# An attention and channel-mix kernel: the last but one input group of its head loaded and cast in halves, and casting loads released one group later

## The chip, the cores and the metric

The kernel runs on one core of a Trainium2 chip. The metric is the device time of the program in microseconds (us), as the median of several executions. The profile shows one execution; its span is about 1.8 us shorter than the time of the same execution, so spans are compared with spans and times with times.

The engines are PE (TensorE, matrix products), PEld (its weight loads), DVE (VectorE), ACT (ScalarE), POOL (GpSimd) and SP (SyncE, which here only issues transfers).

## The reference

Two layers run one after the other, with B = 4, N = 6208, C = 256 and a hidden width of 1024:

```python
# cross-covariance attention
qn = q / (norm(q, axis=1) + 1e-6);  kn = k / (norm(k, axis=1) + 1e-6)
s  = kn.transpose(0, 2, 1) @ qn / tau          # 256 x 256 for each batch
a  = softmax(s, axis=-1)
x  = v @ a
# channel mix
xk = mu_k * x + (1 - mu_k) * x_prev            # x_prev: x shifted by one row
xr = mu_r * x + (1 - mu_r) * x_prev
out = sigmoid(xr @ w_r) * (relu(xk @ w_k)**2 @ w_v)
```

The softmax of a batch needs all rows of its q and k. So batch 0's q and k have to be read first: this is the *head*. From then on (the *body*) the kernel works on blocks of 512 rows of v and takes the sums of the next batch along.

## The kernel before

Rows are taken in groups of 512: twelve of them (`NB = 12`; g = 0 to 11, called k0 to k11 and q0 to q11 below) and a rest of 64 rows (k12). A k piece of the head is a load in fp32, a cast to bf16 on DVE, squares on ACT, products on PE, and one piece later the sums of the squares on PE:

```python
def k_piece(g, s0, s1, last=False):            # s0:s1 of the four 128-row parts of group g
    f = head_load(k, 0, g, s0, s1)             # DMA issued by SP; 8 buffers
    kt = pq.tile([P, S, C], BF16, name="kb", tag="kb", bufs=6)
    nc.vector.tensor_copy(kt[:rows, :n], f[:rows, :n])                 # L141, the cast
    sq = ...
    nc.scalar.activation(sq[:rows, :n], f[:rows, :n], AF.Square)       # L143
    ...  nc.tensor.matmul(s_ps0[:, ih, :], kt[...], qb[g][...])        # L146, s += k^T q
    flush()                                    # L113: norm matmuls of the piece before
```

A q piece looks the same, without the products but with `filler(FQ, g)`: three matmuls (L192) whose result nobody reads, which keep PE busy. The order in the head, and the lines that the change edits:

```python
order += [("k", NB)] + [("k", g) for g in range(NB - LEAD, NB - 1)]   # k12, k4 ... k10
for what, g in order:
    ...
        kt = k_piece(g, 0, rows_of(g)[1])
        ...
        if g == NB - LEAD + 2:
            nc.vector.tensor_copy(rq_bc0, bc_ps)       # the q norms; used by the softmax
        if g == NB - 2:                                # after k10
            nc.sync.dma_start(mu_k_t, ...)             # 2 x 256 values of 4 bytes
            nc.sync.dma_start(mu_r_t, ...)
        if g == NB - 5:                                # k7: the gate
            nc.gpsimd.tensor_copy(gate, kt[:, 0, 0:1]) # POOL waits here for k7's cast ...
            v_load(0)                                  # ... and then issues the casting loads
            nc.gpsimd.dma_start(w_k_sb, ...)
            v_load(1); v_load(2); more_rows(1)
k_piece(NB - 1, 0, 2)                                  # k11 in three pieces
k_piece(NB - 1, 2, 3)
k_piece(NB - 1, 3, 4, last=True)
flush()
```

After the head come the softmax (L157 opens it), the transposes of v's first two blocks on PE (L247), the first block's x (L273), and then the body, which opens with block 0's products with w_k (L339) and block 1's x matmul (L258).

Of the kernel before, what the change touches and what calls it, by code (L numbers as in the profile page):

```python
# [18 lines left out]
def kernel(  # L19
# [21 lines left out]
    NB = N // M  # L41
# [40 lines left out]
    def rows_of(g):  # L82
        return (P, S) if g < NB else (L, 1)
# [5 lines left out]
    LEAD = 8  # L89
# [3 lines left out]
    def head_load(t, b, g, s0, s1):  # L93
        rows = rows_of(g)[0]
        f = pq.tile([P, S, C], F32, name="f", tag="f4", bufs=NF)
        nc.sync.dma_start(f[:rows, :s1 - s0], src_rows(t, b, g, s0, s1))
        return f
# [6 lines left out]
    def first(key):  # L104
        if key in started:
            return False
        started.add(key)
        return True
# [9 lines left out]
    def flush():  # L118

        while pend:  # L120
            norm_mm(*pend.pop(0))

    def q_piece(g, last=False):
        rows, n = rows_of(g)
        f = head_load(q, 0, g, 0, n)
        qt = pq.tile([P, S, C], BF16, name="qb", tag="b2", bufs=NB + 1)
        qb[g] = qt
        nc.vector.tensor_copy(qt[:rows, :n], f[:rows, :n])
        sq = pq.tile([P, S, C], BF16, name="hsq", tag="hsq", bufs=5)
        nc.scalar.activation(sq[:rows, :n], f[:rows, :n], AF.Square)  # L130
        flush()
        pend.append((nq_ps, "q", sq, rows, n, last))
        if g < NB:
            filler(FQ, g)

    def k_piece(g, s0, s1, last=False):
        rows, n = rows_of(g)
        n = s1 - s0
        f = head_load(k, 0, g, s0, s1)
        kt = pq.tile([P, S, C], BF16, name="kb", tag="kb", bufs=6)  # L140
        nc.vector.tensor_copy(kt[:rows, :n], f[:rows, :n])  # L141
        sq = pq.tile([P, S, C], BF16, name="hsq", tag="hsq", bufs=5)
        nc.scalar.activation(sq[:rows, :n], f[:rows, :n], AF.Square)  # L143
        for s in range(n):
            for ih in range(2):
                nc.tensor.matmul(s_ps0[:, ih, :], kt[:rows, s, ih * P:(ih + 1) * P], qb[g][:rows, s0 + s, :],  # L146
                                 start=first("s"), stop=last and s == n - 1, skip_group_check=True)
        flush()
        pend.append((nk_ps, "k", sq, rows, n, last))
        return kt  # L150

    def root(src, n):
        a = pn.tile([P, 4], F32, name="nrm_a")
        if len(src.shape) == 3:
            nc.vector.tensor_reduce(a[:, :n], src, axis=AX, op=OP.add)
        else:
            nc.vector.tensor_copy(a[:, :n], src)  # L157
        r = pn.tile([P, 4], F32, name="nrm_r")
        nc.gpsimd.tensor_tensor(r[:, :n], a[:, :n], half[:, :n], op=OP.pow)
        return r  # L160

    def inverse(r, n):

        nc.vector.tensor_scalar_add(r[:, :n], r[:, :n], 1e-6)
        o = pn.tile([P, 4], F32, name="nrm_o")
        nc.vector.reciprocal(o[:, :n], r[:, :n])
        return o
# [3 lines left out]
    def spread(r):  # L171
        w = pn.tile([P, 3, 2], BF16, name="rw", bufs=1)
        d = pn.tile([P, 2], F32, name="rd", bufs=1)
        nc.vector.tensor_copy(w[:, 0], r[:, :2])
        nc.vector.tensor_tensor(d, r[:, :2], w[:, 0], op=OP.subtract)
        nc.vector.tensor_copy(w[:, 1], d)
        nc.vector.tensor_tensor(w[:, 2], d, w[:, 1], op=OP.subtract)
        return w

    def broadcast(w, tag, **kw):  # L180
        bc_ps = ps.tile([P, 2, P], F32, name="bc_ps", tag=tag, **kw)
        for h in range(2):
            for u in range(3):
                nc.tensor.matmul(bc_ps[:, h], w[:, u, h:h + 1].to_broadcast([P, P]), ident,
                                 start=h == 0 and u == 0, stop=u == 2, skip_group_check=True)
        return bc_ps.rearrange("p h d -> p (h d)")
# [37 lines left out]
    def v_load(i):  # L224
        b, t = blocks[i]
        v_bf = pq.tile([P, S, C], BF16, name="v_bf", tag="b2", bufs=NB + 1)
        nc.gpsimd.dma_start(v_bf, v[b, t * M:(t + 1) * M, :].rearrange("(s p) c -> p s c", p=P))  # L227
        st[i, "v"] = v_bf
# [184 lines left out]
    def group_load(b, g):  # L413
        rows, n = rows_of(g)
        qk = pq.tile([P, S, 2, C], BF16, name="qk", tag="qk", bufs=5)
        groups[b, g] = {"qk": qk}
        for i, t in enumerate((q, k)):
            nc.gpsimd.dma_start(qk[:rows, :n, i], src_rows(t, b, g))  # L418
# [112 lines left out]
    def more_rows(n):  # L531
        while pos["load"] < min(len(loads), n):
            group_load(*loads[pos["load"]])
            pos["load"] += 1

    loads = [(b, g) for b in range(1, B) for g in GORD]
    order = [("q", NB)] + [("q", g) for g in range(LEAD)]
    for g in range(LEAD, NB):
        order += [("k", g - LEAD), ("q", g)]
    order += [("k", NB)] + [("k", g) for g in range(NB - LEAD, NB - 1)]  # L540
    for what, g in order:
        if what == "q":
            q_piece(g, last=g == NB - 1)
        else:
            kt = k_piece(g, 0, rows_of(g)[1])
            if g == NB:
                nq = root(nq_ps, 2)
            if g == NB - LEAD + 1:
                bc_ps = broadcast(spread(inverse(nq, 2)), "v", bufs=2)
            if g == NB - LEAD + 2:  # L550
                nc.vector.tensor_copy(rq_bc0, bc_ps)
            if g == NB - 2:
                nc.sync.dma_start(mu_k_t, moe_mu_k.rearrange("(h p) -> p h", p=P))
                nc.sync.dma_start(mu_r_t, moe_mu_r.rearrange("(h p) -> p h", p=P))
            if g == NB - 5:
                nc.gpsimd.tensor_copy(gate, kt[:, 0, 0:1])
                v_load(0)
                nc.gpsimd.dma_start(w_k_sb, moe_w_k.rearrange("(ko ki) f -> ki ko f", ki=P))
                v_load(1)
                v_load(2)  # L560
                more_rows(1)
    k_piece(NB - 1, 0, 2)
    k_piece(NB - 1, 2, 3)
    k_piece(NB - 1, 3, 4, last=True)
# [40 lines left out]
    for i in range(-2, NBLK):  # L605
        for j in range(8):
# [58 lines left out]
            for u in due.get(T, []):  # L665
                b, g, s = units[u]
# [48 lines left out]
```

## Time and profile before

| | before |
|---|---|
| time, median of 3 | 511.66 us (511.42 to 511.71) |
| span of the profiled execution | 509.72 us |
| PE busy | 493.9 us, 97% |
| first matmul of k7 to last norm matmul of k | 32.78 to 38.64 us |
| last norm matmul of k to block 1's first x matmul | 7.03 us |
| block 1's first x matmul to the last matmul of all | 459.53 us |

Beside what the prediction quotes, three views are needed for the comparison, the third behind the prediction. The first is PE's timeline at the end of the head (start in us, duration, engine, line, operation, out and inputs, sizes, number of instructions):

```profile
34.74 0.34 PE L113 MATMUL nk_ps<-ones_b,hsq 128*128 128x1 bf16 x8
...
35.82 0.34 PE L113 MATMUL nk_ps<-ones_b,hsq 128*128 128x1 bf16 x8
36.30 1.05 PE L146 MATMUL s_ps<-qb,kb 128*128 128x256 bf16 x8
```

The eight norm matmuls take 0.20 us of PE's issue (34.74 to 34.95, where the next group starts: no pause). After those of 35.82 the next group, k10's, starts only at 36.30: this is the hole of which the prediction speaks. The second view is PE's timeline where the body opens:

```profile
43.66 0.62 PE L247 MATMUL vT_ps<-ident,v_bf 128*128 128x128 bf16 x8 [0.21 <-DMA v_bf<-in_v_dram]
...
44.98 0.59 PE L339 MATMUL kT_ps<-xk,w_k_sb 128*128 128x512 bf16 x2
45.66 0.39 PE L258 MATMUL xT_ps<-vT,a_sb 128*128 128x512 bf16 x1
```

PE waits for v1's landing; from there its own instructions run on to block 1's x matmul at 45.66. The third is a row of SP's own waits in the last 5 us: the wait for the last stores of the result, us in total, times, longest.

```profile
SPq L710 <- DMA out_dram<-res: 1.8, 1, 1.8
```

### The profile page before, as it was taken

Reading aid. Unit: us, or ns where it says so; the run is one execution under the profiler, and the core shown is the slowest. Engines: PE = TensorE matmul, PEld = TensorE weight load, DVE = VectorE, ACT = ScalarE, POOL = GpSimd, SP = SyncE. Lnnn points to the kernel's source line nnn. Section 1 sums busy time; section 2 is a strip of 40 time slices with the busy share of each in tenths; the row PEclk is TensorE's granted clock in tenths of the full one; section 3 lists DMA queues with packets and bytes.
Section 4 is the critical chain, followed back from the end, with each engine's and each line's share of the span. In section 5 each row is a group of like instructions: output and inputs, shape, how many; then the busy total and the mean of one; then the engine's idle time right before and its main releaser. Section 6 shows DMA issues by size and latency. Waiting matters only on the chain. (4 is left out here: it accounts for less than half of the span.)

```text
span 509.7 us, 9775 instructions
## 1 busy us (share of the span) xinstructions
PE 493.9 (97%) x3722; PEld 339.3 (67%) x3722; DVE 444.7 (87%) x703; ACT 431.8 (85%) x816; POOL 106.2 (21%) x145
## 2 busy tenths in 40 slices
PE   5799999999999999999999999999999999999996
PEld 2474677777676776677666667667666666666675
DVE  3467798999999999999999999999998787878884
ACT  5777999999998998998998899899787777787773
POOL 0047433332531321221341132100121100000000
PEclk9999999999999999999999999999999999999999
DMA  8999999999999999899699999962298764332213
GB/s 310 398 333 191 180 200 205 201 204 199 186 208 158 217 164 129 166 159 154 128 177 193 157 217 159 146 133 67 62 175 140 119 130 116 75 105 62 72 53 104
DMA packets 143199, 83.48 MB, mean 164 GB/s; under 512 B 51184, under 2 KB 139824, under 8 KB 143152
## 3 DMA queue, kind: packets, MB, share of 16 engines
q0 software_dynamic: 65808, 33.01, 52.5%
q1 hardware_dynamic: 77184, 49.72, 42.0%
q8 instruction: 29, 0.48, 0.4%
q10 hardware_dynamic: 160, 0.13, 0.1%
q14 instruction: 18, 0.15, 0.1%
HBM read 78.71 MB, written 25.43 MB: 204 GB/s over the span
## 5 line engine op out<-in xcount | busy, mean ns | idle before, releaser
L343 ACT ACTIVATE kr<-kT_ps 128x512 bf16<-128x512 f32 (+1 forms) x392 | 232.8, 597 | 36.6 <-PE kT_ps L339 28.7
L339 PE MATMUL kT_ps<-xk,w_k_sb 128*128 128x512 bf16 (+1 forms) x784 | 231.5, 377 | 0.5 <-DVE xk L324 0.5
L389 PE MATMUL v_ps<-w_v_sb,kk 128*128 128x256 bf16 x1536 | 230.4, 273 | 0.0
L389 PEld LDWEIGHTS <-kk 128*128 128x128 bf16 x1536 | 150.2, 98 | 57.6
L350 DVE TENSOR_TENSOR kk<-kr 128x1024 bf16<-128x1024 bf16 (+1 forms) x196 | 132.6, 680 | 34.4 <-ACT kr L343 33.7
L433 ACT ACTIVATE sq<-qk 128x512 f32<-128x512 bf16 (+1 forms) x147 | 93.5, 636 | 0.0
L339 PEld LDWEIGHTS <-w_k_sb 128*128 128x128 bf16 x784 | 75.1, 98 | 22.1 <-issue 1.0
L360 PE MATMUL g_ps<-w_r_sb,xr 128*128 128x256 bf16 x388 | 73.9, 273 | 0.0
L324 DVE SCALAR_TENSOR_TENSOR xr<-delta,mu_r_t,X 128x512 bf16<-128x512 bf16 x96 | 71.2, 744 | 0.0
L260 ACT CAST X<-xT_ps 128x512 bf16<-128x512 f32 x94 | 55.6, 591 | 18.5 <-PE xT_ps L258 17.7
L360 PEld LDWEIGHTS <-xr 128*128 128x128 bf16 x388 | 37.9, 98 | 45.5 <-issue 1.3
L324 DVE SCALAR_TENSOR_TENSOR xk<-delta,mu_k_t,X 128x512 bf16<-128x512 bf16 x94 | 66.1, 744 | 0.0
L402 DVE SCALAR_TENSOR_TENSOR res<-res,v_ps 128x512 f32<-128x512 f32 x96 | 65.2, 679 | 0.0
L418 POOL DMA_DIRECT2D qk<-in_q_dram x39 | 28.6, 733 | 153.0 <-ACT sq L433 123.6
L395 ACT ACTIVATE res<-g_ps 128x512 f32<-128x512 f32 x97 | 57.9, 597 | 0.4 <-PE g_ps L360 0.4
L258 PE MATMUL xT_ps<-vT,a_sb 128*128 128x512 bf16 x188 | 55.9, 379 | 0.3 <-ACT vT L251 0.2
L429 PE MATMUL s_ps<-qk 128*128 128x256 bf16 (+1 forms) x294 | 56.1, 272 | 0.0
L227 POOL DMA_DIRECT2D v_bf<-in_v_dram x48 | 36.9, 771 | 59.9 <-DMA vT<-v_bf 49.7
L464 DVE TENSOR_TENSOR acc<-acc,sq 128x1024 f32<-128x1024 f32 x32 | 39.0, 1220 | 1.0
L429 PEld LDWEIGHTS <-qk 128*128 128x128 bf16 (+1 forms) x294 | 27.4, 98 | 12.3 <-issue 1.3
L313 DVE TENSOR_TENSOR delta<-X 128x1024 bf16<-128x1024 bf16 x48 | 32.9, 685 | 0.1
L418 POOL DMA_DIRECT2D qk<-in_k_dram x39 | 28.8, 739 | 9.1 <-DMA qk<-in_k_dram 3.0
(74 smaller groups left out, 243.0 us busy)
## 6 DMA issues: line engine op xcount, KB each, us to landing
out_dram<-res SPq DMA_DIRECT2D x48, 512.0 KB, 3.8
v_bf<-in_v_dram POOLq DMA_DIRECT2D x48, 256.0 KB, 8.9
qk<-in_q_dram POOLq DMA_DIRECT2D x36, 256.0 KB, 9.7
qk<-in_k_dram POOLq DMA_DIRECT2D x36, 256.0 KB, 10.1
f<-in_q_dram SPq DMA_DIRECT2D x12, 512.0 KB, 8.2
f<-in_k_dram SPq DMA_DIRECT2D x11, 512.0 KB, 9.1
vT<-v_bf SPq DMA_TRANSPOSE x44, 7.6
w_k_sb<-in_moe_w_k_dram POOLq DMA_DIRECT2D x1, 512.0 KB, 8.1
```

Of the source, the lines that this page charges most:

```text
L258: nc.tensor.matmul(xT_ps, a_sb[:, b, ih, dh * P:(dh + 1) * P], vT[:, :, ih, :], start=ih == 0, stop=ih == 1)
L324: nc.vector.scalar_tensor_tensor(o[:, dh], st[i, "d"][:, dh], mu[:, dh:dh + 1], X[:, dh, c:c + M], op0=OP.mult, op1=OP.add)
L339: nc.tensor.matmul(kT_ps[:, :m], w_k_sb[:, dh, fh * P:(fh + 1) * P], xk[:, dh, :m], start=dh == 0, stop=dh == 1)
L343: nc.scalar.activation(st[i, "kr", fh // 2][:, fh % 2, :m], kT_ps[:, :m], AF.Relu, scale=RH)
L350: nc.vector.tensor_tensor(st[i, "kk"][:, fh - 1:fh + 1, :m], kr[:, :, :m], kr[:, :, :m], op=OP.mult)
L360: nc.tensor.matmul(g_ps[:, s % 2], xr[:, dh, s * P:(s + 1) * P], w_r_sb[:, dh, :], start=s % 2 == 0 and dh == 0, stop=dh == 1, skip_group_ ...
L389: nc.tensor.matmul(v_ps[:, s % 2], kk[:, fh, s * P:(s + 1) * P], w_v_sb[:, fh, :], start=s % 2 == 0 and fh == 0, stop=fh == 7, skip_group_ ...
L395: nc.scalar.activation(st[i, "res"][:, 2 * u:2 * u + 2], st.pop((i, "g", u)), AF.Tanh, scale=0.5)
L402: nc.vector.scalar_tensor_tensor(r, r, 1.0, st.pop((i, "v", u)), op0=OP.add, op1=OP.mult)
L418: nc.gpsimd.dma_start(qk[:rows, :n, i], src_rows(t, b, g))
L429: nc.tensor.matmul(cov[b][:, ih, :], qk[:rows, s, 1, ih * P:(ih + 1) * P], qk[:rows, s, 0, :], start=g == GORD[0] and s == 0 and ih == 0, ...
L433: nc.scalar.activation(G["sq", s // 2][:rows, s % 2], qk[:rows, s], AF.Square)
```

## The change

The intent is to let PE begin k10 when half of it is cast, and to move the casting loads' descriptor work out of the way of the casts. (Descriptor work is the name here for POOL's DMA_DIRECT2D instructions, 0.73 to 0.91 us each for v0, w_k, v1 and v2 in before; what POOL does in them is not shown.) The diff:

```diff
-    order += [("k", NB)] + [("k", g) for g in range(NB - LEAD, NB - 1)]
+    order += [("k", NB)] + [("k", g) for g in range(NB - LEAD, NB - 2)]
 ...
-            if g == NB - 2:
+            if g == NB - 4:
                 nc.sync.dma_start(mu_k_t, moe_mu_k.rearrange("(h p) -> p h", p=P))
                 nc.sync.dma_start(mu_r_t, moe_mu_r.rearrange("(h p) -> p h", p=P))
-            if g == NB - 5:
+            if g == 8:
                 nc.gpsimd.tensor_copy(gate, kt[:, 0, 0:1])
 ...
+    k_piece(NB - 2, 0, 2)
+    k_piece(NB - 2, 2, 4)
     k_piece(NB - 1, 0, 2)
     k_piece(NB - 1, 2, 3)
     k_piece(NB - 1, 3, 4, last=True)
```

It has three parts: the halves of k10; the gate at k8's cast instead of k7's; and the two mu loads between k8 and k9 instead of between k10 and k11. The third follows from the first: k10 is no longer in the loop in which the mu loads hang.

## The prediction

> **What bounds the kernel now.** I read the page's busy table and slices first, then busy time by stretch, then the timeline of the first 55 us engine by engine, then the landings of the transfers.
>
> ```profile
> PE 493.9 (97%) x3722; PEld 339.3 (67%) x3722; DVE 444.7 (87%) x703; ACT 431.8 (85%) x816; POOL 106.2 (21%) x145
> PE   5799999999999999999999999999999999999996
> ...
> 30.00:40.00 10.00, 9.79 (x142) 8.47 (x142) 6.75 (x17) 7.34 (x10) 5.75 (x9) 1.00 1.07 270
> 40.00:50.00 10.00, 9.52 (x49) 3.83 (x48) 8.20 (x19) 8.06 (x18) 8.15 (x11) 1.00 1.43 195
> ...
> 100.00:300.00 200.00, 199.78 (x1476) 138.88 (x1474) 193.39 (x295) 182.07 (x363) 55.94 (x73) 1.00 1.22 176
> ```
>
> The stretch rows give busy us of PE, PEld, DVE, ACT, POOL, then clock, DMA share, GB/s. From 100 to 300 us PE is busy 199.78 of 200: the body is a PE stream which this change doesn't touch. Only the head (to about 45 us) is edited, so the time moves by as much as the start of the body moves, and the whole question is a few tenths of a us in 511.66.
>
> With N = 6208 there are twelve 512-row groups, k0 to k11, and a 64-row rest. The head loads q and k of batch 0, casts on DVE, squares on ACT, and accumulates on PE. Its end:
>
> ```profile
> 33.84 0.88 DVE L141 CAST kb<-f 128x1024 bf16<-128x1024 f32 x1 [0.51 <-DMA f<-in_k_dram]
> 34.95 1.03 PE L146 MATMUL s_ps<-qb,kb 128*128 128x256 bf16 x8
> 35.21 1.03 DVE L141 CAST kb<-f 128x1024 bf16<-128x1024 f32 x1 [0.50 <-DMA f<-in_k_dram]
> 36.30 0.77 PEld L146 LDWEIGHTS <-kb 128*128 128x128 bf16 x8 [0.23 <-DVE kb L141]
> ...
> 38.84 0.16 DVE L157 COPY nrm_a<-nk_ps 128x2 f32<-128x2 f32 x1 [1.63 <-PE nk_ps L113]
> ```
>
> Columns: start, duration, engine, line, operation, idle before. These are k9's cast, k9's matmuls, k10's cast, k10's first weight load, and the norm that opens the softmax. Matmul by matmul, PE issues without a pause from 32.78 to 38.66, but for one hole: k8's last norm matmul starts at 35.99 (next slot 36.02) and k10's first at 36.30, since k10's cast ends only at 36.24. The hole is 0.28 us, and it is the most that halving k10 can win: after it PE is the queue, and the k11 pieces wait for PE.
>
> Why is k10's cast 1.03 us when the casts at 28.23 to 32.64 take 0.68 to 0.69? It lies beside descriptor work on POOL:
>
> ```profile
> 32.79 0.58 POOL L556 COPY gate<-kb 128x1 bf16<-128x1 bf16 x1 [3.24 <-DVE kb L141]
> 33.31 0.91 POOL L227 DMA_DIRECT2D v_bf<-in_v_dram  x1
> 34.23 0.73 POOL L558 DMA_DIRECT2D w_k_sb<-in_moe_w_k_dram  x1
> 34.94 1.61 POOL L227 DMA_DIRECT2D v_bf<-in_v_dram  x2
> ```
>
> The gate copy, released by k7's cast, opens the casting loads (v0, w_k, v1, v2). The last view is what happens after the head:
>
> ```profile
> 43.65 0.45 PEld L247 LDWEIGHTS <-v_bf 128*128 128x128 bf16 x8 [0.70 <-DMA v_bf<-in_v_dram]
> ...
> mu_k_t<-in_moe_mu_k_dram SPq DMA_DIRECT2D x1, 1.0 KB, 7.9
> mu_r_t<-in_moe_mu_r_dram SPq DMA_DIRECT2D x1, 1.0 KB, 7.6
> ```
>
> PE waits again at 43.65 for v1 (landed 43.61). And w_v lands at 51.35 while PE's first use of it starts at 51.52. So two transfers from the gated queue sit on or beside PE's path after the head.
>
> [...] 0.88 us and 1.03 us beside descriptor work against 0.68 clear. [...] k10, mu_k, mu_r, k11 land in issue order (35.19, 35.37, 35.55, 35.96). [...] Here the 128x256 cast takes 0.27 us undisturbed against 0.68 for 128x1024, so by a straight line (estimate) the fixed part is 0.14 and a 512-wide one 0.41: a split adds about 0.14 on DVE. On ACT the squares are 1.06, 0.61 and 0.40 us for 1024, 512 and 256, so the split adds 2 x 0.61 - 1.06 = 0.16.
>
> **The change, part by part.**
>
> (1) *k10 in halves.* One more load, cast and square, no more matmuls. DVE's extra 0.14 lies where DVE idled 0.50 us per group; ACT's 0.16 where it idled 0.31. k10's first half can be cast before k9's matmuls are over, so the 0.28 hole goes. Gain at most 0.28.
>
> (2) *The mu loads come two groups earlier.* The order listing shows a part that the title doesn't name: mu_k and mu_r were issued between k10 and k11 and are now between k8 and k9. They are 2 x 256 packets of 4 bytes. Cost: k10 to k11's first half took 35.96 - 35.19 = 0.77 us, where half of the usual 1.28 us interval is 0.64, so at least 0.13; the two landings are 0.18 apart, so at most 0.36. In the middle 0.25 (estimate). It doesn't move the end of k11, but k9 lands 0.25 later: 33.81 + 0.25 = 34.06.
>
> (3) *Gate after k8's cast instead of k7's.* Those casts end at 32.73 and 33.33, so the gate copy starts at 33.39, 0.60 later, and the descriptor work runs from 33.91. k9's cast (34.09) is now wholly beside it and should take about 1.03, like k10's before: it ends at 35.12, and k9's matmuls start about 0.06 later, at 35.18 instead of 34.95.
>
> *Sum for the head.* PE's work from k9's first matmul to the last norm is 38.66 - 34.95 - 0.28 = 3.43 us. 35.18 + 3.43 = 38.61, against 38.66: 0.05 earlier. With a cheap mu and a less disturbed k9 cast it is the full 0.28 earlier; with mu at 0.36 and 1.03 us it is 35.29 + 3.43 = 38.72, 0.06 later. The halves then only repay what (2) and (3) take at k9.
>
> *After the head.* v0 landed at 37.92 with its transposes starting at 38.66. A 0.60 delay at its issue partly disappears[...]; I expect 38.1 to 38.5, just in time. v1 and w_k: the packet records show the first 512-byte packets of v1 starting at 39.3 while the last 2048-byte ones of w_k start at 41.8[...]. [...] v1 at about 43.6, w_v at about 51.4. If so, v1's wait swallows most of any head gain: PE would merely wait longer at 43.65, and only what doesn't stand behind v1 (the two x evacuations of block 0) moves, at most 0.2. I take 0.1 of gain as the middle: 511.66 - 0.1 = 511.5 to 511.6.
>
> **The rivals.**
>
> *The hole's gain arrives in full.* For it: PE's path from 36.30 to the softmax is unbroken, and the body is all PE. Against: the v1 wait at 43.65. It would give 511.66 - 0.28 = 511.4, a little less if the quieter queue also lands v1 sooner.
>
> *The later gate takes the wait's place.* For it: with the gate 0.60 later, [...] v1 comes at 44.2 and w_v at 51.95. PE would hold at 43.65 and again at 51.52, and some 0.4 to 0.6 would pass into the body: 512.1 to 512.3. Against: [...]the DMA share of 1.43 in 40 to 50 us, where the queue is full anyway.
>
> *k is transfer-bound.* The extra small packets and the 2 KB pieces could slow the last loads. k11's last piece landed at 36.60 and PE reached it at 38.34, 1.7 us later, so this would need a delay of over 1 us; nothing speaks for that.
>
> **Range and chances.** The body's 460 us are the same instructions in the same order, so 2% (10 us) is out of reach unless something falls over. The three runs of before span 0.29 us, and parts (1) to (3) span from -0.28 to +0.6. I set 511.5, 511.0 to 512.1; faster by 2% 0.005, slower by 2% 0.005.
>
> **What would show it.** Right: k10's first matmul directly behind k9's norms, without a hole; mu landing before k9, k9 about 0.25 later; k9's cast near 1 us, with a new wait of PE for it near 35; v1's landing within 0.2 of 43.6 and PE's wait for it as long or longer. Wrong: k9 landing at 33.8 as before, so that the head ends 0.28 sooner; v1 or w_v landing 0.4 or more later, with PE idle before them; v0 later than PE's arrival; or a body that runs slower with an unchanged head, which nothing here explains.

The head's sum: 35.18 + 3.43 = 38.61 against 38.66, so 0.05 us earlier, from -0.28 to +0.06. For the time, 0.1 us of gain was taken as the middle: 511.66 - 0.1 = 511.5 to 511.6, set at 511.5 (511.0 to 512.1). v1 and w_v should land as before (43.61 and 51.35), and v0's delay of 0.60 us should partly disappear: both stand as assumptions. That no more than 0.2 us of the head's gain arrives, with 0.1 as the middle, rests on the first of them.

## The result, and the profile after

| | before | after |
|---|---|---|
| time, median (same set of runs) | 511.65 us (511.42 to 511.71, 4 runs) | 511.77 us (511.71 to 511.80, 4 runs) |
| span of the profiled execution | 509.72 us | 510.01 us |
| k7, k8, k9 landed | 31.21, 32.49, 33.81 | 31.30, 32.80, 34.25 |
| k9's cast | 0.88 us | 0.95 us |
| last norm matmul of k starts | 38.64 | 38.69 |
| v0 landed, v1 landed | 37.92, 43.61 | 38.57, 42.36 |
| block 1's first x matmul | 45.66 | 45.73 |

The ratio of the times is 1.0003, with a 95% interval of 0.9986 to 1.002: the same. The time is inside the predicted range, 0.27 us above the middle.

The page's busy row:

```profile
PE 493.2 (97%) x3722; PEld 339.2 (67%) x3722; DVE 444.8 (87%) x704; ACT 431.8 (85%) x817; POOL 105.9 (21%) x145
```

There is one more instruction on DVE (x704 against x703) and one on ACT (x817 against x816): the extra cast and square. PE has the same 3722. The busy times of the engines by stretch (PE, PEld, DVE, ACT, POOL, then clock, DMA share, GB/s):

```profile
30.00:40.00 10.00, 9.81 (x141) 8.49 (x141) 6.82 (x19) 7.33 (x11) 5.39 (x9) 1.00 1.05 266
40.00:50.00 10.00, 9.50 (x48) 3.93 (x47) 8.21 (x19) 7.97 (x18) 8.21 (x11) 1.00 1.40 189
100.00:300.00 200.00, 199.78 (x1476) 138.89 (x1475) 193.38 (x296) 182.07 (x363) 55.94 (x73) 1.00 1.20 177
```

The body's PE time, 199.78 of 200 us, is that of before to the last digit. Now PE's timeline at the end of the head:

```profile
34.82 0.34 PE L113 MATMUL nk_ps<-ones_b,hsq 128*128 128x1 bf16 x8
35.28 1.05 PE L146 MATMUL s_ps<-qb,kb 128*128 128x256 bf16 x8
36.16 0.34 PE L113 MATMUL nk_ps<-ones_b,hsq 128*128 128x1 bf16 x8
36.37 0.60 PE L146 MATMUL s_ps<-qb,kb 128*128 128x256 bf16 x4
...
38.61 0.24 PE L113 MATMUL nk_ps<-ones_b,hsq 128*128 128x1 bf16 x4
```

The hole has moved by one group. k10 (36.37, in the half form x4) follows its predecessor after the usual 0.21 us, but k9 starts at 35.28 where it could have started at 35.02: a wait of 0.26 us. What sets it is k9's cast, in DVE's timeline:

```profile
34.27 0.95 DVE L141 CAST kb<-f 128x1024 bf16<-128x1024 f32 x1 [0.76 <-DMA f<-in_k_dram]
...
38.89 0.16 DVE L157 COPY nrm_a<-nk_ps 128x2 f32<-128x2 f32 x1 [1.48 <-PE nk_ps L113]
```

The cast starts 0.44 us later than before, as k9 landed 0.44 later, and takes 0.95 us (0.88 before). It lies beside v0's descriptor work, as POOL's timeline shows:

```profile
33.58 0.18 POOL L556 COPY gate<-kb 128x1 bf16<-128x1 bf16 x1 [3.95 <-DVE kb L141]
33.83 0.91 POOL L227 DMA_DIRECT2D v_bf<-in_v_dram  x1
```

The issues of the mu loads (size, median us from issue to landing):

```profile
mu_k_t<-in_moe_mu_k_dram SPq DMA_DIRECT2D x1, 1.0 KB, 8.2
mu_r_t<-in_moe_mu_r_dram SPq DMA_DIRECT2D x1, 1.0 KB, 7.1
```

They landed at 32.97 and 33.15, between k8 and k9. And the opening of the body on PE:

```profile
43.34 0.61 PE L247 MATMUL vT_ps<-ident,v_bf 128*128 128x128 bf16 x8
...
44.66 0.85 PE L339 MATMUL kT_ps<-xk,w_k_sb 128*128 128x512 bf16 x2
45.73 0.39 PE L258 MATMUL xT_ps<-vT,a_sb 128*128 128x512 bf16 x1 [0.23 <-ACT X L285]
```

This is the first surprise. v1 landed 1.25 us earlier and PE no longer waits for it: the transposes start 0.32 us sooner than before. Yet the x matmul starts 0.07 us *later*, since PE now waits 0.23 us for ACT's copy of X (L285), which depends on block 0's chain and not on v1. ACT's timeline of before shows that the same copy came last there too:

```profile
45.04 0.59 ACT L285 CAST X<-xT_ps 128x512 bf16<-128x512 f32 x1 [0.28 <-DVE xk L280]
```

It ends at 45.63, 0.03 us ahead of the x matmul (after: 45.70 and 45.73). So PE did wait for v1 in before, but that wait was over early enough to cost the x matmul nothing. From there on the two kernels run in step: matmul by matmul, the body of the changed kernel lies a constant 0.07 us later for 450 us.

The second surprise is at the end. The head accounts for 0.07 us, but the span grew by 0.29. SP's wait for the last stores:

```profile
SPq L712 <- DMA out_dram<-res: 2.1, 1, 2.1
```

It is 0.3 us longer. The records of the last microsecond show why. SP ends by passing eight pairs of waits, one pair for each of eight completion semaphores that the transfers of SP and ACT use, in the same order in both profiles and some 0.06 us apart. The last stores are two of SP's and two of ACT's; the one that lands last is ACT's.

```
                                   before        after
SP's last two stores landed        508.264       508.326
                                   508.437       508.499
  they complete the                1st, 2nd      2nd, 3rd pair
ACT's last store landed            508.610       508.671
  it completes the                 8th           1st pair
1st pair passed at                 508.281       508.687
2nd pair passed at                 508.454       508.749
walk over the pairs done           508.849       509.143
last landing to walk done            0.239         0.472
```

Before, SP waits at the first two pairs for its own two stores and then walks on without a stop; ACT's store lands meanwhile, long before the walk comes to the eighth pair. After, SP stands at the first pair until ACT's store has landed, and the whole walk is still ahead of it. The semaphores go to the transfers in turn: in both profiles the first 30 landings on them (to 36.60 us before, 36.49 after) fall on the first to the eighth and begin anew, and there are 130 of them in all before and 131 after. The changed kernel has one more load, so each later transfer uses the next semaphore: SP's last two stores move from the first and second semaphore to the second and third, and ACT's last store from the eighth to the first, as the turn begins again there. So far this is two profiles; the experiments had to confirm it.

### The profile page after: what moved, and what is told of

Same layout as the page of the kernel before. It is cut to its first block, busy times and chain, and to the rows that moved or that the text cites. A ratio compares the mean times of both kernels' runs of the same rounds, so it can differ in the third digit from the quotient of the medians. Undisturbed runs are those within 1.5% of the kernel's fastest.

```text
span 510.0 us, 9781 instructions
## 1 busy us (share of the span) xinstructions
PE 493.2 (97%) x3722; PEld 339.2 (67%) x3722; DVE 444.8 (87%) x704; ACT 431.8 (85%) x817; POOL 105.9 (21%) x145
```

## The experiments

The theory after this reading: (1) what follows the last norm matmul is rigid, so only the head's end counts; (2) the halves gain k10's hole; (3) the earlier mu loads and k9's slow cast give it back. Its rivals are the prediction's: v1's landing swallows what the head gains, or the later gate takes away by its own late loads. All twelve runs gave right results. Kernels run together share their runs of before. Where a run has a "norm" time, it is the start of the last norm matmul of k in the profiled execution, and "waits" is the time that PE stood between k7's first matmul and that norm: their distance less 5.55 us, which is the smallest that any profile shows.

### First set: each part alone

The runs of before in this set: 511.72 (511.43 to 515.51, 11 runs).

**e1_split_only: the halves alone.** The mu loads stay between k10 and k11, the gate stays at k7.

```diff
-    order += ... range(NB - LEAD, NB - 1)]
+    order += ... range(NB - LEAD, NB - 2)]
-            if g == NB - 2:  (both mu loads)
+    k_piece(NB - 2, 0, 2)
+    k_piece(NB - 2, 2, 4)
+    (both mu loads)
     k_piece(NB - 1, 0, 2)
```

> k10 in halves alone; mu between k10 and k11 and the gate at k7's cast, as in the kernel before. Theory A (the end of the k chain on PE sets the softmax, and that sets a rigid body): k9's matmuls start at 34.95 as before, the hole of 0.28 us before k10's matmuls is gone, the last norm and with it block 1's first x matmul (45.66 before) come 0.28 us sooner, 45.38, and the time falls by 0.2 to 0.3 us to about 511.4. Rival B (my prediction: v1's landing at 43.61 holds PE and swallows the gain): the chain ends 0.28 sooner, but block 1's first x matmul moves by 0.1 or less and the time stays within 0.1 of before.

Measured: 511.73 (511.32 to 512.86, 6 runs), ratio 0.9988 (0.9965 to 1.0012). The profile fell on an execution with a disturbance that I had not seen before: its span is 511.09. By stretch (columns as above):

```profile
22.20:25.60 3.40, 1.95 (x27) 1.20 (x25) 1.39 (x2) 1.90 (x2) 0.00 (x0) 1.00 1.03 369
26.00:28.00 2.00, 2.00 (x24) 1.34 (x22) 0.89 (x2) 1.78 (x3) 0.00 (x0) 0.50 1.02 404
```

The granted PE clock fell to 0.50 at 25.7 us, and stayed there for 3.41 us. PE was busy all of 26 to 28 us and got through 24 matmuls (in before 32, in 1.96 us), k7's first matmul came at 34.24 instead of before's 32.79, and PE was late enough never to wait for a cast again. So this profile can't tell what the halves gain. It does show block 1's x matmul 7.03 us after the norm, although both came over 1.1 us later than in before: the rigidity holds. And it shows the tail: 0.473 us from the last landing to the end of the walk.

**e2_mu_only: the mu loads alone.**

```diff
-            if g == NB - 2:
+            if g == NB - 4:
                 (both mu loads)
```

> The mu loads issued after k8 instead of after k10, alone. Theory A (the small packets ahead of k9 are what the change lost): k8 lands near 32.8 and k9 near 34.25 (32.49 and 33.81 before), k9's matmuls start at 35.2 to 35.3, k10 is still whole, lands near 35.6 and leaves its hole, so that the chain ends 0.25 to 0.4 later than before and the time rises by that: 511.9 to 512.1. Rival C (the packets cost nothing, and the lateness of k8 and k9 in the changed kernel came from its other parts): k9 lands within 0.1 of 33.81, time as before.

Measured: 511.81 (511.57 to 512.94), ratio 0.999 (0.9967 to 1.0013), norm at 38.84. PE's timeline:

```profile
35.92 0.34 PE L113 MATMUL nk_ps<-ones_b,hsq 128*128 128x1 bf16 x8
36.51 1.05 PE L146 MATMUL s_ps<-qb,kb 128*128 128x256 bf16 x8 [0.24 <-DVE kb L141]
```

k9 landed 2.85 us after k7, against 2.60 in before, and the hole before k10 grew from 0.28 to 0.38 us. k10 too landed later (4.29 us after k7, against 3.98), and only its quicker cast, 0.77 us instead of 1.03, kept the loss small. k9's cast took 0.69. In this execution the part costs about 0.1 us by itself. v1 landed at 42.11 here, 1.5 us earlier than in before, and x still stood 7.03 us after the norm: against the rival.

**e3_gate_only: the gate alone.**

```diff
-            if g == NB - 5:
+            if g == 8:
```

> The gate at k8's cast instead of k7's, alone. Theory A: k9's cast lies wholly beside descriptor work and takes about 1.0 us, but it starts at 33.84 and PE comes to it only at 34.95, so nothing moves: chain end within 0.1 of before, time 511.6 to 511.7. Theory D (the gate is what brought v1 from 43.61 to 42.36 in the changed kernel): v1 lands at 42.4 to 42.8 here and not in the other single parts. Rival E (the gate costs time: v0 comes late): v0 lands after 38.66 and the body starts 0.2 or more later.

Measured: 511.53 (511.47 to 512.94), ratio 0.9987 (0.9961 to 1.0013), norm at 38.64. k9's cast, which I expected near 1 us, took 0.69. First POOL's timeline, then DVE's:

```profile
33.82 1.18 POOL L227 DMA_DIRECT2D v_bf<-in_v_dram  x1
```

```profile
33.99 0.69 DVE L141 CAST kb<-f 128x1024 bf16<-128x1024 f32 x1 [0.49 <-DMA f<-in_k_dram]
```

The descriptor work of v0 took 1.18 us here instead of the 0.91 of before and after, so this time POOL paid for the overlap. v0 landed at 38.46, v1 at 42.51: the later gate did not make the landings that count late. In this profile waits are 0.13 us, 0.11 of it before k10.

**e4_split_gate: the halves and the gate, mu loads left late.** The edits of e1 and e3 together.

> The change without its move of the mu loads: halves and the later gate, mu between k10 and k11. Theory A: k9 lands at 33.81 again, its cast may take 1.0 but ends by 34.9, no hole after it: chain end 0.28 before that of the kernel before (38.38 instead of 38.66), unless v0 is not there by then: it landed at 38.57 in the changed kernel, and if it does so here, PE's transposes and the ACT copies behind them start at about 38.6 and the gain is 0.05 to 0.1. Time 511.4 with v0 in time, 511.55 to 511.6 with v0 late. Rival B (v1 holds the body): no gain if v1 lands at 43.6.

Measured: 511.74 (511.39 to 512.81), ratio 0.999 (0.9966 to 1.0014). PE's timeline:

```profile
35.85 0.34 PE L113 MATMUL nk_ps<-ones_b,hsq 128*128 128x1 bf16 x8
36.05 0.60 PE L146 MATMUL s_ps<-qb,kb 128*128 128x256 bf16 x4
...
38.30 0.24 PE L113 MATMUL nk_ps<-ones_b,hsq 128*128 128x1 bf16 x4
```

Nothing waits from k7 to the end. The norm starts at 38.38, 0.26 us earlier than in before, and block 1's x matmul at 45.41, 0.25 earlier: the hole's gain does arrive in the body in full. The last matmul is earlier by 0.225 us (504.966 against 505.191). And the span is 509.73, that of before: the 0.23 us went to the walk at the end, which took 0.47 us after the last landing. This run separates the head from the tail.

### Second set: repeats, and one copy moved

The runs of before: 511.75 (511.52 to 513.31, 11 runs). To see what differs from execution to execution, before and after were profiled once more (one timed run each, so of unknown state):

**e5_before_again**: no edit.

> The kernel before, unchanged, for a second profile: how much of what I read as a difference is the luck of one execution. If v1's landing at 43.61 belongs to the kernel it is there again; if it was chance it lands at 42.0 to 42.6 as in the four single-part runs. k9's cast was 0.88 us; it may be 0.69 here. Block 1's first x matmul should stand 7.03 to 7.04 us after the last k norm matmul, and the last matmul 459.5 us after that, as in all six profiles so far. Chain end 38.6 to 38.8.

Measured: 512.27, span 510.49. Again the clock halved for 3.41 us in the head, at 23.8, after PE had stood waiting for a cast for 2.05 us until 23.05. Three fillers (L192) that started at 24.58, in that stretch, took 1.44 us; the next three, at 27.75, took 0.81. v1 landed at 42.67. So its landing at 43.61 in the first profile of before was luck of that execution, not a property of the kernel. x stood 7.03 us after the norm all the same.

**e6_after_again**: no edit of the changed kernel.

> The changed kernel, unchanged, for a second profile. Theory A: mu ahead of k9 again makes k9 land near 34.25; if its cast is slow again (0.9 to 1.0) PE waits before k9's matmuls until about 35.3 and the chain ends near 38.7; if the cast is 0.69 the chain ends 0.25 sooner, near 38.45. So the changed kernel's loss against the split alone would be part mu, part the luck of cast against descriptor work.

Measured: 512.26, span 510.49. The input stream was about half a us late from the start (k7 landed at 31.83 instead of 31.30), and the end of the head with it (norm at 39.16). Otherwise it repeats the first profile: k9 landed 2.88 us after k7, its cast took 0.96, and PE waited 0.19 us in the chain, most of it before k9.

The next two test another way to k9. A copy of the q norms on DVE (`rq_bc0`) stands in the stretch before k7; moved behind the last cast of k, it should let the casts run on.

**e7_split_rq**: e1, with the copy moved.

```diff
-            if g == NB - LEAD + 2:
-                nc.vector.tensor_copy(rq_bc0, bc_ps)
 ...
     k_piece(NB - 1, 3, 4, last=True)
+    nc.vector.tensor_copy(rq_bc0, bc_ps)
```

> A version meant to beat both: k10 in halves, mu and gate as in the kernel before, and the copy of the q norms out of PSUM moved behind k11's last cast on DVE, because it stood in front of k7's cast and left a hole of 0.23 us on PE before k7's matmuls. Theory A: both holes go, the last norm comes 0.45 to 0.5 us before that of the kernel before (38.64), at about 38.15, v0 (37.9 to 38.0) is there, block 1's first x matmul comes 7.03 later, at about 45.2, and the time in undisturbed runs falls by 0.4 to 0.5 to about 511.15. Rival: v0 or the ACT copies of its transpose now end after the softmax's norm, and only 0.3 arrives.

Measured: 511.64 (511.34 to 515.07, 6 runs), ratio 1.0002 (0.9979 to 1.0024), span 509.96: not the gain expected. The stream was 0.47 us late in the profiled execution (k7 landed at 31.68). From k7's landing to the norm it took 7.02 us, against 7.43 in before (and 7.10 in e10 below, the halves without the moved copy), so the edit does what it should behind k7; but the tail took 0.47 instead of 0.24, and the stream's own jitter is larger than what is left.

**e8_split_gate_rq**: e4, with the copy moved.

> The same with the gate at k8's cast. Theory A: v0 lands near 38.4 (38.37 in the run with halves and gate), after the last norm at about 38.17, so PE's transposes wait for it and the ACT copies of them end after the norm is ready: the body starts only 0.25 to 0.35 before that of the kernel before, at 45.3 to 45.4, worse than with the gate at k7 by 0.1 to 0.2. Rival: the later gate is harmless and both versions are equal.

Measured: 514.05 (511.94 to 515.34, 6 runs), ratio 1.0036 (1.001 to 1.0062): the one kernel with a clear loss, if a small one. Its profile (span 511.29) has the half clock at 25.6 for 3.41 us. Every run of it shows a mean granted clock of 0.987 to 0.996, where most runs of the others show 0.997 to 1.0; the three runs above 515 show 0.987. One stretch of 3.41 us at half clock lowers the mean over 510 us by 0.5 x 3.41 / 510 = 0.0033, so 0.987 would be some four of them (an estimate). Why this kernel meets them so often stays open.

### Third set: more fillers, to see whether the clock still falls

The runs of before: 511.59 (511.49 to 512.84, 9 runs). In the three profiles with half clock PE was busy 1.95, 1.35 and 1.91 us of the 3.40 us ahead of the drop. In other profiles stretches as long with 1.75 us (e3) and 1.81 us (after) were followed by none, so this share alone doesn't decide it. The edit doubles the fillers behind the q pieces with long waits:

```diff
-            filler(FQ, g)
+            filler(6 if LEAD <= g < NB - 1 else FQ, g)
```

**e9_fq_only**: before, with this edit.

> The kernel before with six instead of three filler matmuls after q8, q9 and q10, nothing else. Theory F (three of ten profiles, e1, e5 and e8, show TensorE at half clock for 3.41 us starting between 23.7 and 25.7, after a stretch in which PE idled; each of these heads ended about 1 us late, and the runs over 512.4 us are such runs): PE is busy 65 to 75% of that stretch instead of 45 to 55%, no half clock before 40 us, at most one run of six over 512.2 (about a third of the runs of before are), median 511.5 to 511.7. Rival: the half clock comes whatever PE does, and two or three of six runs are over 512.2 as before.

Measured: 511.44 (511.28 to 511.66, 5 runs), ratio 0.9992 (0.9979 to 1.0004), span 509.66. The stretch ahead of e1's drop is now busier:

```profile
22.20:25.60 3.40, 2.72 (x31) 1.79 (x32) 2.02 (x3) 2.90 (x3) 0.00 (x0) 1.00 1.03 367
```

2.72 of 3.40 us, and the clock stays at 1.00. There was no hole before k10 in this execution although k10 was whole: its cast took 0.69 us instead of 1.03, and the two v instructions on POOL beside it 2.00 instead of 1.61. POOL paid again.

**e10_split_fq**: e1, with the fillers.

> k10 in halves alone, with those fillers, because the first run of the halves alone fell on a half clock. Theory A: last k norm 7.1 us after k7's landing (7.43 in the kernel before, 7.13 with halves and the later gate), no hole between k9's norms and k10's matmuls; the time in undisturbed runs 0.3 below e9, about 511.3. Rival B (v1 swallows it): block 1's first x matmul less than 6.9 or more than 7.1 us after the last norm, and time equal to e9.

Measured: 511.74 (511.58 to 511.94), ratio 0.9998 (0.9985 to 1.001), span 510.00. I had expected a gain of 0.3 on e9; it is 0.30 above it. In the profiles the difference is 0.34: nothing from the hole, as e9 happened to have none; 0.15 from a stream that ran later (k7 at 31.58 against 31.43); 0.23 from the tail. These make 0.38; a few hundredths came back in the chain.

**e11_split_gate_fq**: e4, with the fillers.

> Halves and the later gate, mu between k10 and k11, with those fillers. Theory A: like e10 within 0.1, last norm 7.1 us after k7's landing unless v0, 0.4 later than in e10, comes after it. Theory G (the later gate is worth something by itself): 0.1 or more below e10.

Measured: 511.87 (511.55 to 512.01), ratio 0.9999 (0.9986 to 1.0012). The profile is of the lowest of its five runs (span 509.78): norm at 38.46, no waits. Here v0 landed late (38.64), and its first transpose started at 38.68, 0.20 us later than it could have. That cost nothing: block 1's x matmul stands 7.04 us after the norm as in the others. This profile is also the plainest test of what v1's landing costs, as v1 landed at 43.62, as late as in the first profile of before (43.61). PE's timeline:

```profile
43.66 0.62 PE L247 MATMUL vT_ps<-ident,v_bf 128*128 128x128 bf16 x8 [0.39 <-DMA v_bf<-in_v_dram]
...
45.50 0.60 PE L258 MATMUL xT_ps<-vT,a_sb 128*128 128x512 bf16 x2
```

PE waited 0.39 us for v1, longer than the 0.21 of before, and still the x matmul came 0.16 us earlier, for a norm 0.18 earlier. Why its median is 0.3 us above the run that was profiled isn't shown.

**e12_after_fq**: the changed kernel, with the fillers.

> The changed kernel with those fillers: against e11 it differs by the place of the mu loads alone. Theory A: k8 and k9 land 0.2 to 0.45 later relative to k7, the last norm comes 7.3 to 7.4 us after k7's landing, 0.2 to 0.3 later than in e11, and the time of undisturbed runs is above e11 by about that, near 511.6. Rival C (the place of mu doesn't matter): within 0.05 of e11.

Measured: 512.07 (511.83 to 512.30), ratio 1.0004 (0.999 to 1.0017), span 510.29. It differs from e11 by the place of the mu loads alone and is 0.20 us above it. k9 landed 2.88 us after k7, its cast took 0.98, and PE waited 0.25 us before k9.

### What the twelve show together

| | k10 | mu loads | waits from k7 to the norm, us | k9 after k7, us | last landing to end of walk, us |
|---|---|---|---|---|---|
| before | whole | late | 0.30 | 2.60 | 0.24 |
| e2 | whole | early | 0.40 | 2.85 | 0.24 |
| e3 | whole | late | 0.13 | 2.59 | 0.24 |
| e9 | whole | late | 0 | 2.58 | 0.24 |
| e4 | halves | late | 0 | 2.60 | 0.47 |
| e10, e11 | halves | late | 0 | 2.61, 2.59 | 0.47 |
| e7 | halves | late | 0.08 | 2.61 | 0.47 |
| after, e6, e12 | halves | early | 0.28, 0.19, 0.26 | 2.95, 2.88, 2.88 | 0.47 |

(e1, e5 and e8 have no waits, as their half clock made PE late; their walks are 0.47, 0.24 and 0.47.) In all fourteen profiles block 1's first x matmul starts 7.03 to 7.05 us after the last norm matmul and the last matmul of all 459.53 to 459.57 us after that, while v1 landed anywhere from 41.93 to 44.14. The last column goes with the halves without exception; no run has the extra transfer without them, so it is the order of the semaphores, and not a run of its own, that ties the longer walk to the transfer.

The half clock is a matter of its own. Of the 31 runs of before in the three sets nine took over 512.4 us; of the 20 runs of the four kernels with more fillers none did (the longest took 512.30). In eight of the nine and in the profiled ones the mean clock is 0.996 or less, one shows 0.997. (One long run of e4, 512.81 at 0.999, is of another kind.) The kernel before has it, so the change does not bring it; the changed kernel's five runs without extra fillers happen to be free of it. It is larger than all that the change does. With medians of five or six runs it also explains why medians here scatter by a few tenths.

## Why the prediction was right or wrong

The time (511.77) lies in the range (511.0 to 512.1). That is partly luck: the range was 1.1 us wide, a gain of 0.1 us was expected where 0.12 us was lost (neither is clear of the noise), and of the larger part of the loss the prediction knew nothing. By its steps:

- **"PE is the body; only the start of the body moves the time."** Right for the body, which repeats to 0.04 us in fourteen profiles. But it left out the other end of the kernel: the tail added 0.23 us, more than the head did. This is the step that failed in the sum, and no part of the prediction came near it. e4 shows it most plainly: the last matmul 0.225 us earlier, the span unchanged.
- **(1) "Gain at most 0.28", the hole before k10.** Right. No halved kernel waits before k10 (0.015 us at most), and e4's norm is 0.26 us earlier.
- **(2) mu loads, k9 0.25 us later.** The mechanism was right; the size was 0.24 to 0.35 (k9 after k7: 2.85 to 2.95 us, against about 2.60 in the undisturbed kernels without the move), and 0.35 in the profile that is compared. I had counted the wait behind the mu loads alone, but they hit k8 too: k8 came 1.44 to 1.49 us after k7 instead of 1.27 to 1.30, although the mu loads are issued behind it.
- **(3) k9's cast near 1.03 us because of the later gate.** Near enough in size for the changed kernel (0.95, 0.96, 0.98), but the gate alone does not do it. With the gate late and the mu loads in their old place (e3, e4, e11) the cast took 0.69 us and v0's instruction on POOL 1.18 to 1.19; with the mu loads early and the old gate (e2) it took 0.69 too. Nor is a slow cast of k9 new: with both in their old places it took 0.88 (before), 0.89 (e9), 0.92 (e7) and 0.84 us (e10), but it ended before PE came to it (in e7 PE waited 0.08 us). What decides is when the cast starts within v0's instruction. Where it started 0.42 to 0.56 us into it (before, after, e6, e9, e10, e12), its end was that of a cast of 0.69 us held back until 0.71 us into the instruction, in all six to within 0.01. Starting 0.71 us in (e2), it lost nothing. Starting 0.18 to 0.20 us in (e3, e4, e11), it ran freely and POOL's instruction took 0.27 to 0.28 us longer. The later gate moves the end of the hold about 0.5 us later (v0's instruction starts at 33.83 instead of 33.31), and the mu loads bring k9's cast into the stretch that is held; of these moves only both together made PE wait at k9, by 0.17 to 0.26 us (e6, e12, after). What happens 0.71 us into the instruction is not shown.
- **Sum for the head: 38.61, from -0.28 to +0.06.** On that mark, the start of what follows the norms, it was 38.72 against 38.66, so 0.06 later: the end of the range. k9's matmuls came at 35.28 where 35.18 was predicted: k9 landed 0.19 later than predicted (34.25 against 34.06; 0.09 of it from a stream that ran later, 0.10 from the mu loads), and its cast was 0.08 shorter than the 1.03 assumed.
- **"v1's wait swallows most of any head gain."** Wrong. In e11 v1 landed as late as in before (43.62) and the x matmul was earlier by 0.16 us for a norm 0.18 us earlier; in e4, where v1 came early (42.51), by 0.25 for 0.26. The wait at 43.65 was real but not the one that ends last: that is the wait for ACT's X, in before as in after. v1's landing was predicted at 43.6, within 0.2; it was 42.36, and it scatters over 2.2 us in the fourteen profiles, over 0.9 us in the two of before. I took one execution's landing for a property of the kernel.
- **v0 at 38.1 to 38.5, just in time.** 38.57, with no wait for it, though 0.65 us later than before for an issue 0.52 later (33.83 against 33.31), so no part of the delay disappeared; and where it did make PE wait (e11), that cost nothing.
- **Rivals.** "The gain arrives in full" holds for the head of e4, not for the changed kernel. "The later gate takes the wait's place" fell: no profile shows PE held at the body's opening by a later landing. "k is transfer-bound" in the form put there fell too, though its remark on small packets was the right place to look.

What the change does to the profiled execution is, then: the halves take away the 0.28 us before k10, the mu loads and the later gate, by k9's late landing and slow cast, put 0.26 us before k9, the stream happened to run 0.09 us later, and so the body starts 0.07 us later; the walk at the end adds 0.23. The sum is 0.30, and the spans differ by 0.29. The medians differ by 0.12, inside the jitter of the stream.

A version that I would try next leaves the mu loads late, halves k10, and loads k11 in two pieces instead of three, so that the number of transfers stays as it is. From e4 and the walk it should gain about 0.25 us (an estimate: e4's 0.26 without the longer walk), if two pieces of k11 cost PE nothing. It was not run. None of those run beats before by more than the noise.

## What to carry to other kernels

Before crediting a wait with swallowing a gain, ask whether it is the last one to end on that path, and whether its time repeats: one profile gives one execution's landings (v1's lay between 41.93 and 44.14 here). A change in the head can cost at the tail (0.23 us here), so compare both ends of the two traces, last matmul against last matmul and last landing against end of span. And a part that moves along by accident, like two tiny loads that hang on a loop index, can give back what the intended part gains (here, with the later gate, 0.26 of 0.28 us).
